# Layer 2's output product by Strassen's scheme: seven block products where there were eight

## The chip, the core and the metric

The kernel runs on one core of a Trainium2 chip. The metric is the device time of one execution in microseconds (us). Three runs of the kernel before gave 1030.38, 1031.73 and 1032.31 us; the median is 1031.73 us. The execution that the profiler recorded took 1031.0 us. Its span, from the first to the last instruction in the trace, is 1029.2 us, so 1.8 us of it lie outside the span.

Five engines work side by side, each with its own queue of instructions that it takes in order: PE (matrix products; a second row, PEld, lists its loads of the stationary operand), DVE (vector), ACT (scalar functions), POOL (general) and SP (issues the DMA transfers). Products are summed in PSUM, a small memory from which DVE and ACT read the result.

## The reference

Three stages run one after the other on 8 batches of 576 tokens. Attention with 8 heads over keys and values that are averaged in groups of 8 gives x with 512 features per token. Two gated layers follow. Layer 1:

```
h = relu(x @ w_in);  u, v = h[:, :512], h[:, 512:]       # w_in 512 x 1024
v_n = (v - mean(v)) / sqrt(var(v) + 1e-6)                # over the 512 features
v_s = w_spatial @ v_n + b_spatial                        # over the 576 tokens
x = (u * v_s) @ w_out                                    # w_out 512 x 512
```

Layer 2 has the same shape with other weights, a tanh form of GELU in place of relu, a gain on v_n, and the input added at the end: `x + gated @ w_out`. That last line is the product that is changed.

## The kernel before

**Numbers.** Every fp32 value that enters a product is split in two, a high part hi (rounded by ACT, L152) and a low part lo = value - hi (by DVE, in places by POOL, L153). A product is three products summed in one PSUM tile: hi by hi, hi by lo, lo by hi.

**Blocks.** A layer runs batch by batch, in blocks with one letter each in the strings that give the order. The layer's output is kept with features on the partitions (128 of them per tile) and 576 tokens along the row.
- `v`: 128 tokens by 512 features of the second half of h (`emit_v`, 12 matmuls of 512 columns, L252 to L254). Its chain on the other engines is GELU (L286, L287, L290, L291), the statistics (L300, L301, POOL L305 to L310), the gain (L321), hi (ACT L328) and lo (DVE L313). `v4` holds the last 64 tokens of two batches and so comes every second batch; its lo parts are 64 x 512.
- `u`: 128 features by 576 tokens of the first half (`emit_u`, L357, 24 matmuls of 288 columns), then GELU (L369, L370, L373, L374).
- `p`: the product with w_spatial for 128 features (`emit_sp`, L389, 28 matmuls of 288 columns). DVE multiplies it with u (L398) and the result gf is split into g (L152, L153).
- `o`: 128 output features (`emit_out`, L411, 4 feature chunks x 3 terms x 2 token halves = 24 matmuls of 288 columns). In layer 2 DVE adds the residual tile r (L422) and SP stores the result (L423). In layer 1 ACT copies it (L418) and SP stores it to x2d in DRAM, from which layer 2 loads it (`load_x`, `L`), splits it (`split_x`, `X`, lo on POOL) and gathers the last 64 tokens of two batches (`rem_x`, `R`).
- `G` loads and splits one of four 128 x 512 pieces of layer 2's w_out (`load_w2_out`), `I` pieces of its w_in, `E` its spatial weights.

**Order.** The emission order of layer 2 is written out in strings: PH2 for a batch in the steady state (the o blocks are those of the batch before), BOUND for the change from layer 1 to layer 2 and TAIL for the last batch. A scheduler keeps that as the order of priority on every engine, and a tile's number of buffers decides what waits: three PSUM tiles of two banks for u, p and o together, two PSUM tiles for v.

Of the kernel before, what the change touches and what calls it, by code (L numbers as in the profile page):

```python
# [32 lines left out]
SLAG = 0  # L33
LAG = {1: 4, 2: 2}
# [49 lines left out]
def attention_gmlp_gmlp(  # L84
# [40 lines left out]
    x2d = [[dram.tile([P, S], F32, name=f"x2d{b}_{c}") for c in range(NC)] for b in range(B)]  # L125
# [119 lines left out]
    seen = set()  # L245
    jobs_left = [2 * NC]
# [9 lines left out]
    def emit_v(layer, b, xt, t, pools, lag=1):  # L256
# [60 lines left out]
        def norm():  # L317
            if layer == 1:
                nc.vector.tensor_scalar(v[:m], v[:m], mv[:m, 0:1], None, ALU.subtract)
            else:  # L320
                nc.vector.scalar_tensor_tensor(  # L321
                    out=v[:m], in0=v[:m], scalar=mv[:m, 0:1], in1=pools["g"][:m],
                    op0=ALU.subtract, op1=ALU.mult,
                )
            if t < 4:
                o = pools["vn"].tile([P, 2, DH], F32R, tag="vn", name="vn")
                vn[b, t] = o
                nc.scalar.activation(out=o[:, 0], in_=v[:m], func=AF.Copy, scale=rstd[:m])  # L328
                lo_part(o[:, 1], o[:, 0], 0, m)
            elif not pair:  # L330
                hi = vna[b % 2][:m]
                nc.scalar.activation(out=hi, in_=v[:m], func=AF.Copy, scale=rstd[:m])
                nc.scalar.activation(out=vnx[b % 2][:m], in_=v[:m], func=AF.Copy, scale=rstd[:m])
                lo_part(vnx[b % 2][64:], hi, 0, m)
            else:
                hi = pools["h"].tile([P, DH], F32R, tag="h", name="h")
# [13 lines left out]

    def emit_u(layer, b, xt, d, pools):
        ps = ps_b.tile([P, 2, 512], F32, tag="b", name="pu")
        ds_ = slice(d * P, (d + 1) * P)
        for c in range(NC):
            for i, (w, hl) in enumerate(((wih, 0), (wih, 1), (wil, 0))):
                for h in range(2):
                    nc.tensor.matmul(  # L357
                        out=ps[:, h, :HALF], lhsT=w[c][:, ds_],
# [7 lines left out]
        else:  # L366
            sq = pools["w"].tile([P, S], F32, tag="squ", name="squ")
# [10 lines left out]
    def emit_sp(layer, b, d, pools):  # L378
        ps = ps_b.tile([P, 2, 512], F32, tag="b", name="psp")
        ds_ = slice(d * P, (d + 1) * P)  # L380
        seq = []
        for t in range(4):
            hi, lo = vn[b, t][:, 0, ds_], vn[b, t][:, 1, ds_]
            seq += [(hi, wsh[t]), (hi, wsl[t]), (lo, wsh[t])]
        seq.append((vna[b % 2][:97, ds_], wsa[:97]))
        seq.append((vnx[b % 2][:, ds_], wsx))
        for i, (l, r) in enumerate(seq):
            for h in range(2):
                nc.tensor.matmul(  # L389
                    out=ps[:, h, :HALF], lhsT=l, rhs=r[:, h * HALF:(h + 1) * HALF],  # L390
# [14 lines left out]
    def emit_out(layer, b, m, pools):  # L405
# [26 lines left out]
    if True:  # L432
# [34 lines left out]
        def mlp1(tok):  # L467
# [551 lines left out]
        w_p = ctx.enter_context(tc.tile_pool(name="w", bufs=2))  # L1019
        g_p = ctx.enter_context(tc.tile_pool(name="g", bufs=1))  # L1020
        r_p = ctx.enter_context(tc.tile_pool(name="r", bufs=8))
        xr_p = ctx.enter_context(tc.tile_pool(name="xr", bufs=2))
        h_p = ctx.enter_context(tc.tile_pool(name="h", bufs=1))
        staging.update(pool=ctx.enter_context(tc.tile_pool(name="stage", bufs=3)), tag="raw", n=S)
        gb = g_p.tile([P, DH], F32, name="gb")
        nc.sync.dma_start(out=gb, in_=g_ln.to_broadcast([P, DH]))
        pools.update({"w": w_p, "g": gb, "res": {}, "xr": {}, "h": h_p})
# [12 lines left out]
        def rem_x(b):  # L1040
            raw = xr_p.tile([P, NC, P], F32, tag="xw", name="xw")
            for i in range(2):
                for c in range(NC):
                    nc.sync.dma_start(out=raw[:, c, 64 * i:64 * i + 64], in_=x2d[b + i][c][:, 4 * P:])
            xr = xr_p.tile([P, 2, NC, P], F32R, tag="xr", name="xr")
            split(xr[:, 0], xr[:, 1], raw[:], nc.gpsimd)
            pools["xr"][b] = xr

        def mlp2(tok):
# [96 lines left out]
```

## Time and profile before

| what | value |
|---|---|
| median of three runs | 1031.73 us |
| profiled execution, and its span | 1031.0 us, 1029.2 us |
| PE busy over the span | 990.8 us (96%) |
| DVE, ACT, POOL busy | 669.4, 445.7, 441.9 us (65, 43, 43%) |
| DMA, mean rate over the span | 81 GB/s |
| clock granted to PE, mean of the run | 0.985 |

Attention and layer 1 take the first half of the span. Layer 1 of the last batch and layer 2 of the first overlap between about 490 and 575 us; from there to 1006 us layer 2 runs batch after batch, and the last 23 us are the last batch's output product. A share over the whole span mixes these stages, so the stages are shown apart in the rows below. Clock 1.00 means the upper one of PE's two levels, 2.4 GHz.

### The profile page before, as it was taken

The numbers are of one execution on the slowest core, as the hardware profiler recorded it, in microseconds if no ns is written. First come the engines' busy times: TensorE is split into PE (matmuls) and PEld (weight loads), VectorE is DVE, ScalarE is ACT, GpSimd is POOL, SyncE is SP. The second block draws the span as 40 slices with busy tenths as digits, with TensorE's granted clock in tenths as the row PEclk, the third lists the DMA queues.
The fourth block names the chain that finished last, engine by engine and source line by source line (L and its number), as shares of the span: only waits on it lengthen the run. The fifth ranks groups of instructions, "written<-read, shape, count | busy, mean of one in ns | idle before, by whom it ended". The sixth has DMA issues, their size and how long they took to land.

```text
span 1029.2 us, 17646 instructions
## 1 busy us (share of the span) xinstructions
PE 990.8 (96%) x6752; PEld 939.0 (91%) x6752; DVE 669.4 (65%) x1191; ACT 445.7 (43%) x849; POOL 441.9 (43%) x901
## 2 busy tenths in 40 slices
PE   7589889999999999999999999999999999999998
PEld 6469779999999999999999999999999999999998
DVE  5898867677676776766643477656665665556552
ACT  5564645435354353443533555333434343334330
POOL 4687657484674744714313234233322332232210
PEclk9689999999999999999999999999999999999999
DMA  8533343243332422222014312202011111111001
GB/s 276 169 122 107 121 130 111 88 122 97 104 100 77 138 70 66 83 70 70 30 44 134 109 56 67 70 24 80 24 48 46 48 46 46 46 47 47 12 13 69
DMA packets 49339, 83.00 MB, mean 81 GB/s; under 512 B 14052, under 2 KB 17124, under 8 KB 49256
## 3 DMA queue, kind: packets, MB, share of 16 engines
q1 hardware_dynamic: 49256, 81.89, 25.5%
q8 instruction: 53, 0.87, 0.4%
q14 instruction: 30, 0.25, 0.1%
HBM read 59.85 MB, written 22.02 MB: 80 GB/s over the span
## 4 chain that ended last, share of the span: by engine, by line
PE 82%; DVE 6%; DMA 4%; POOL 3%; ACT 3%; issue 1%; SPq 0%; POOLq 0%; DVEq 0%; ACTq 0%
PE psp L389 22%; PE pout L411 18%; PE pu L357 17%; PE pv L252 5%; PE pv L254 5%; PE pv L253 5%; PE psc L729 3%; DMA w2d_in<-dtmp 1%; POOL vr L597 1%; PE ptr L790 1%; DMA draw<-in_w_out_dram 1%; PE pv L265 1%; DMA vr<-in_v_dram 1%; PE ppv L252 1%; PE ppv L253 1%
## 5 line engine op out<-in xcount | busy, mean ns | idle before, releaser
L389 PE MATMUL psp<-wsh,vn 128*128 128x288 f32 x1024 | 189.9, 297 | 0.0
L411 PE MATMUL pout<-g,woh 128*128 128x288 f32 x1024 | 179.7, 297 | 2.7 <-DVE g L153 2.6
L357 PE MATMUL pu<-x,wih 128*128 128x288 f32 x1024 | 178.5, 296 | 0.0
L411 PEld LDWEIGHTS pout<-g,woh 128*128 128x128 f32 x1024 | 152.4, 189 | 5.5 <-DVE g L153 2.8
L389 PEld LDWEIGHTS psp<-wsh,vn 128*128 128x128 f32 x1024 | 153.7, 188 | 2.1 <-issue 1.0
L357 PEld LDWEIGHTS pu<-x,wih 128*128 128x128 f32 x1024 | 150.8, 188 | 1.3
L305 POOL TENSOR_SCALAR rs<-mv 128x1 f32<-128x1 f32 (+1 forms) x76 | 34.6, 455 | 189.0 <-DVE mv L301 186.6
L411 PE MATMUL pout<-g,wol 128*128 128x288 f32 x512 | 110.0, 296 | 0.0
L389 PE MATMUL psp<-wsl,vn 128*128 128x288 f32 x512 | 109.7, 295 | 0.0
L357 PE MATMUL pu<-x,wil 128*128 128x288 f32 x512 | 109.2, 295 | 0.0
L252 PE MATMUL pv<-wih,x 128*128 128x512 f32 x256 | 102.8, 402 | 3.0 <-ACT v L283 2.2
L152 ACT ACTIVATE g<-gf 128x576 fp32r<-128x576 f32 x64 | 43.9, 686 | 132.3 <-DVE gf L398 62.4
L254 PE MATMUL pv<-wih,x 128*128 128x512 f32 x256 | 100.9, 394 | 0.0
L253 PE MATMUL pv<-wil,x 128*128 128x512 f32 x256 | 100.6, 393 | 0.0
L153 DVE TENSOR_TENSOR g<-gf,g 128x576 fp32r<-128x576 f32 x64 | 56.3, 880 | 44.7 <-ACT g L152 44.6
L153 POOL TENSOR_TENSOR x<-r,x 128x576 fp32r<-128x576 f32 x32 | 47.5, 1486 | 84.9 <-ACT x L152 84.9
L411 PEld LDWEIGHTS pout<-g,wol 128*128 128x128 f32 x512 | 83.1, 190 | 0.0
L389 PEld LDWEIGHTS psp<-wsl,vn 128*128 128x128 f32 x512 | 82.5, 189 | 0.0
L357 PEld LDWEIGHTS pu<-x,wil 128*128 128x128 f32 x512 | 82.3, 189 | 0.0
L313 DVE SCALAR_TENSOR_TENSOR vn<-v,rs,vn 128x512 fp32r<-128x512 f32 x64 | 51.0, 799 | 43.9 <-ACT vn L328 43.9
L770 POOL TENSOR_TENSOR se<-se,sum 128x576 f32<-128x576 f32 (+1 forms) x35 | 41.9, 1196 | 65.6 <-DVE sum L769 64.9
L328 ACT ACTIVATE vn<-v,rs 128x512 fp32r<-128x512 f32 x64 | 45.7, 717 | 49.4 <-POOL rs L310 47.8
(177 smaller groups left out, 1968.1 us busy)
## 6 DMA issues: line engine op xcount, KB each, us to landing
x2d<-o SPq DMA_DIRECT2D x32, 288.0 KB, 3.0
r<-x2d SPq DMA_DIRECT2D x32, 288.0 KB, 3.1
out_dram<-o SPq DMA_DIRECT2D x32, 288.0 KB, 2.2
q<-in_qm_dram SPq DMA_DIRECT2D x32, 256.0 KB, 3.6
kr<-in_k_dram SPq DMA_DIRECT2D x14, 576.0 KB, 3.7
vr<-in_v_dram SPq DMA_DIRECT2D x28, 256.0 KB, 2.9
raw<-in_w_in_dram SPq DMA_DIRECT2D x8, 512.0 KB, 4.7
draw<-in_w_out_dram SPq DMA_DIRECT2D x16, 256.0 KB, 2.9
```

Source lines behind the costliest of these rows:

```text
L152: nc.scalar.activation(out=hi, in_=src, func=AF.Copy)
L153: (eng or nc.vector).tensor_tensor(out=lo, in0=src, in1=f32(hi), op=ALU.subtract)
L252: nc.tensor.matmul(out=o, lhsT=lh, rhs=rh, start=start and i == 0, stop=False)
L253: nc.tensor.matmul(out=o, lhsT=lh, rhs=rl, start=False, stop=False)
L254: nc.tensor.matmul(out=o, lhsT=ll, rhs=rh, start=False, stop=stop and i == n - 1)
L305: gp.tensor_scalar(a, mv[:m, 1:2], 1.0, eps, ALU.mult, ALU.add)
L313: nc.vector.scalar_tensor_tensor(out=lo, in0=v[r0:r1], scalar=rstd[r0:r1], in1=f32(hi), op0=ALU.mult, op1=ALU.subtract)
L328: nc.scalar.activation(out=o[:, 0], in_=v[:m], func=AF.Copy, scale=rstd[:m])
L357: nc.tensor.matmul(out=ps[:, h, :HALF], lhsT=w[c][:, ds_], rhs=xt[c][:, hl, h * HALF:(h + 1) * HALF], start=c == 0 and i == 0, stop=c == N ...
L389: nc.tensor.matmul(out=ps[:, h, :HALF], lhsT=l, rhs=r[:, h * HALF:(h + 1) * HALF], start=i == 0, stop=i == len(seq) - 1,)
L411: nc.tensor.matmul(out=ps[:, h, :HALF], lhsT=w[c][:, ms], rhs=gt[b, c][:, hl, h * HALF:(h + 1) * HALF], start=c == 0 and i == 0, stop=c == ...
L770: (nc.vector if (b, t) in SM_DVE else nc.gpsimd).tensor_tensor(e3, e3, sm[:m, :, None].to_broadcast([m, 8, SP]), ALU.mult)
```

## The change

The 512 x 512 product of a batch, out = A·B with A the transposed w_out and B the gated tile (features x tokens), is cut into 2 x 2 blocks: A into blocks of 256 x 256, B into blocks of 256 features x 288 tokens. The plain way takes eight block products. Now seven are computed, of sums and differences of blocks:

- S1 = A21+A22, S2 = S1-A11, S3 = A11-A21, S4 = A12-S2 are made once, when the weights are loaded: `load_w2_out` is called twice (before: four times), and each call loads two pieces, makes four 128 x 256 sums on POOL and splits seven 128 x 256 pieces on ACT and DVE.
- T1 = B12-B11, T2 = B22-T1, T3 = B22-B12, T4 = T2-B21 are made for each batch on POOL from the unsplit gf tiles (four 128 x 576 operations), and B11, B21, B22, T1, T2, T3, T4 are split: seven splits a batch, before four.
- The seven products `o0` to `o6` are 2 feature chunks x 3 terms x 2 = 12 matmuls of 288 columns each. Three PSUM tiles hold them. Tile a receives P1, and on top of it P6, P7 and P4 (o0, o2, o4, o6); tile d receives P5 and on top of it P3 (o1, o5); tile b receives P2 (o3). After each product DVE adds what the PSUM tile holds at that moment to one of four residual tiles, in place (seven additions a batch, L499 of the kernel after; before four).
- The residual is loaded from x2d once more for this (`load_r`, four transfers of 288 KB a batch), in blocks of 256 features x 288 tokens, and the stores have the same shape.
- u and p in layer 2 are computed in the same arrangement (`place`): a PSUM tile holds two 128-feature chunks of one token half, where it held two halves of one chunk. Neighbouring matmuls of a pair then have different stationary operands; before they had the same one.
- Layer 2's strings of order are new, and pools have other sizes (w 3, r 3, staging 4, residual 2 + 2, T tiles 2, shared with the tile of `rem_x`).

The core of the diff:

```diff
 PH2 = (
-    "v1 v0 o2 L0 v2 o0 L2 R o1 L3 v4 L1 u3 v3 u1 o3 X0 X1 u0 p1 p0 X3 u2 X2 p2 p3"
+    "o0 L2 v2 o1 L3 L1 v1 R o2 o3 v3 o4 X1 u0 o5 o6 L0 v0 v4 u1 X0 X3 u3 X2 u2 p1 p0 p3 p2"
 )
...
-    def load_w2_out(c):
-        seen.add(("G", c))
-        load_split(w2d_out[c][:, :], woh[c][:], wol[c][:])
+    def load_w2_out(k):
...
+            nc.gpsimd.tensor_tensor(o, x, y, op)
...
+            nc.scalar.activation(out=hi, in_=x, func=AF.Copy, scale=sg)
+            nc.vector.scalar_tensor_tensor(out=lo, in0=x, scalar=sg, in1=f32(hi), op0=ALU.mult, op1=ALU.subtract)
+            wblk[n, k] = hi, lo
...
+    def place(layer, d, j):
+        return (d, j) if layer == 1 else (d // 2 * 2 + j, d % 2)
...
-                for h in range(2):
+                for j in range(2):
+                    dd, h = place(layer, d, j)
                     nc.tensor.matmul(
-                        out=ps[:, h, :HALF], lhsT=w[c][:, ds_],
+                        out=ps[:, j, :HALF], lhsT=w[c][:, dd * P:(dd + 1) * P],
...
+        if layer == 2:
+            gb[b, GN[d]] = g
+            if GN[d] != "B12":
+                split_g(b, GN[d], "xg")
+            for o, x, y in TS:
+                if (b, o) not in gb and (b, x) in gb and (b, y) in gb:
+                    z = pools["t"].tile([P, S], F32, tag="raw", name="tf")
+                    nc.gpsimd.tensor_tensor(z, gb[b, x], gb[b, y], ALU.subtract)
+                    gb[b, o] = z
+                    if o in ("T1", "T2"):
+                        defer(TLAG, lambda o=o: split_g(b, o, "tg"))
+            return
...
+    PRODS = {
+        "5": ("S1", "T1", "d", "22"), "1": ("A11", "B11", "a", "11"), "2": ("A12", "B21", "b", "11"),
+        "6": ("S2", "T2", "a", "12"), "3": ("S4", "B22", "d", "12"), "7": ("S3", "T3", "a", "22"),
+        "4": ("nA22", "T4", "a", "21"),
+    }
...
+    def emit_out2(b, i):
...
+        wn, gn, pn, rn = PRODS[PORD[i]]
+        first = pn not in st
+        if first:
+            st[pn] = ps_b.tile([P, 2, 512], F32, tag="b", name="pout")
+        ps = st[pn]
...
+        for k in range(2):
+            hi, lo = wblk[wn, k]
+            for n, (w, hl) in enumerate(((hi, 0), (hi, 1), (lo, 0))):
+                for j in range(2):
+                    nc.tensor.matmul(
+                        out=ps[:, j, :HALF], lhsT=w[:, j * P:(j + 1) * P], rhs=two(g[:, hl])[:, k],
+                        start=first and k == 0 and n == 0, stop=k == 1 and n == 2,
...
+        if PORD[i] in "56":
+            split_g(b, "T3" if PORD[i] == "5" else "T4", "tg")
+        r = st[rn]
+        nc.vector.tensor_tensor(out=two(r[:]), in0=halves(ps), in1=two(r[:]), op=ALU.add)
...
-            r = pools["res"].pop((b, m))
-            nc.vector.tensor_tensor(out=two(o[:]), in0=halves(ps), in1=two(r[:]), op=ALU.add)
-            nc.sync.dma_start(out=out[b, ms, :], in_=o)
```

Where the instructions move, engine by engine. PE before, the steady state of layer 2: one whole output block `o` (g is the moving operand, woh and wol are the stationary high and low parts of w_out's four pieces).

```order
L411 MATMUL pout_10085<-g_9691,woh0_80 128x288 x4
L411 MATMUL pout_10085<-g_9691,wol0_84 128x288 x2
L411 MATMUL pout_10085<-g_9657,woh1_81 128x288 x4
L411 MATMUL pout_10085<-g_9657,wol1_85 128x288 x2
L411 MATMUL pout_10085<-g_9762,woh2_82 128x288 x4
L411 MATMUL pout_10085<-g_9762,wol2_86 128x288 x2
L411 MATMUL pout_10085<-g_9796,woh3_83 128x288 x4
L411 MATMUL pout_10085<-g_9796,wol3_87 128x288 x2
```

PE after, the same stage: o2 and o3 of one batch with the start of the v block behind them, then o4, the start of a u block, o5 and the start of o6 (pout_9866 is tile a, pout_9916 tile d, pout_9991 tile b; wx holds S2, S3 and S4).

```order
L490 MATMUL pout_9866<-g_9863,wx_6382 128x288 x12
L490 MATMUL pout_9991<-g_9858,woh2_82 128x288 x4
L490 MATMUL pout_9991<-g_9858,wol2_86 128x288 x2
L490 MATMUL pout_9991<-g_9858,woh3_83 128x288 x4
L490 MATMUL pout_9991<-g_9858,wol3_87 128x288 x2
L280 MATMUL pv_10010<-wih0_72,x_9639 128x512
...
L490 MATMUL pout_9866<-g_9933,wx_6382 128x288 x12
L388 MATMUL pu_10057<-x_9639,wih0_72 128x288 x4
...
L490 MATMUL pout_9916<-g_9817,wx_6382 128x288 x12
L490 MATMUL pout_9866<-g_9987,woh2_82 128x288 x4
```

An output block of 24 matmuls became products of 12, and tile a returns in every second one: between o2 and o4 lie o3 and a v block, between o4 and o6 a u block and o5.

DVE before, the steady state, the evacuation of a batch's four p blocks: gating (L398) and the low part (L153) of each, with a u block between the second and the third (L370, L374).

```order
L398 SCALAR_TENSOR_TENSOR gf_10183<-psp_10154,u_10079 128x576
L153 TENSOR_TENSOR g_10185<-gf_10183,g_10185 128x576
L398 SCALAR_TENSOR_TENSOR gf_10217<-psp_10188,u_10148 128x576
L153 TENSOR_TENSOR g_10219<-gf_10217,g_10219 128x576
L370 SCALAR_TENSOR_TENSOR squ_10251<-squ_10251,pu_10225 128x576
L374 SCALAR_TENSOR_TENSOR u_10250<-squ_10251,pu_10225 128x576
L398 SCALAR_TENSOR_TENSOR gf_10288<-psp_10259,u_10250 128x576
L153 TENSOR_TENSOR g_10290<-gf_10288,g_10290 128x576
L398 SCALAR_TENSOR_TENSOR gf_10322<-psp_10293,u_10018 128x576
L153 TENSOR_TENSOR g_10324<-gf_10322,g_10324 128x576
```

DVE after, the same place: the p blocks in the order p1, p0, p3, p2 (L429 gating, L155 low part; tf tiles are differences T made by POOL), and the first additions into the residual tiles (L499), between which the next batch's v blocks stand (L315, L319).

```order
L429 SCALAR_TENSOR_TENSOR gf_9779<-psp_9750,u_9504 128x576
L155 TENSOR_TENSOR g_9781<-gf_9779,g_9781 128x576
L429 SCALAR_TENSOR_TENSOR gf_9815<-psp_9786,u_9670 128x576
L155 TENSOR_TENSOR g_9817<-gf_9815,g_9817 128x576
L155 TENSOR_TENSOR g_9824<-tf_9784,g_9824 128x576
L429 SCALAR_TENSOR_TENSOR gf_9856<-psp_9827,u_9713 128x576
L155 TENSOR_TENSOR g_9858<-gf_9856,g_9858 128x576
L155 TENSOR_TENSOR g_9863<-tf_9820,g_9863 128x576
L499 TENSOR_TENSOR ro_9869<-pout_9866,ro_9869 128x576
L315 SCALAR_TENSOR_TENSOR sq_9900<-sq_9900,pv_9886 128x512
L499 TENSOR_TENSOR rrb_9867<-pout_9916,rrb_9867 128x576
L319 SCALAR_TENSOR_TENSOR v_9899<-sq_9900,pv_9886 128x512
```

The u block's evacuation is gone from between the p blocks, the splits of T1 and T2 came in, and an addition now stands among the next batch's v chain after every 12 matmuls.

## Rows read from the trace of the kernel before

**Rows 1.** Windows: length; busy us (count) PE, PEld, DVE, ACT, POOL; clock; DMA share.

```profile
492.00:575.00 83.00, 83.00 (x581) 79.32 (x580) 40.29 (x79) 34.35 (x65) 22.10 (x59) 1.00 0.21 64
575.00:1006.00 431.00, 431.00 (x2931) 413.13 (x2931) 263.79 (x402) 173.32 (x274) 129.21 (x255) 1.00 0.16 49
1006.00:1029.20 23.20, 19.30 (x145) 19.06 (x144) 6.07 (x8) 0.69 (x1) 0.00 (x0) 1.00 0.20 77
```

**Rows 2.** Windows, one stretch of two batches in layer 2, columns as before.

```profile
693.60:799.20 105.60, 105.60 (x718) 101.14 (x717) 62.49 (x97) 39.71 (x62) 32.18 (x64) 1.00 0.16 48
```

**Rows 3.** The chain that ended last: start us, length us, engine, tile, line, instructions.

```profile
674.50 3.20 PE pu L357 x24
677.70 7.45 PE psp L389 x56
...
704.47 0.24 PE pv L252
...
707.21 6.39 PE pout L411 x48
...
1006.11 19.20 PE pout L411 x144
```

**Rows 4.** Groups by line and shape: count, busy us, mean ns of one, idle before and releaser.

```profile
L411 PEld LDWEIGHTS pout<-g,woh 128*128 128x128 f32 x1024 | 152.4, 189 | 5.5 <-DVE g L153 2.8 <-PE psc L729 0.3
...
L153 DVE TENSOR_TENSOR g<-gf,g 128x576 fp32r<-128x576 f32 x64 | 56.3, 880 | 44.7 <-ACT g L152 44.6
...
L153 POOL TENSOR_TENSOR x<-r,x 128x576 fp32r<-128x576 f32 x32 | 47.5, 1486 | 84.9 <-ACT x L152 84.9
...
L152 ACT ACTIVATE g<-gf 128x576 fp32r<-128x576 f32 x64 | 43.9, 686 | 132.3 <-DVE gf L398 62.4 <-DVE gf L396 54.1 <-PE pu L357 15.8
...
L422 DVE TENSOR_TENSOR o<-pout,r 128x576 f32<-128x576 f32 x32 | 24.0, 749 | 13.1 <-PE pout L411 13.1
...
L597 POOL TENSOR_TENSOR vr<-vr 128x256 f32<-128x256 f32 x24 | 18.2, 759 | 16.6 <-DMA vr<-in_v_dram 12.0 <-DMA draw<-in_w_out_dram 4.4
...
L313 DVE SCALAR_TENSOR_TENSOR vnx<-v,rs,h 64x512 fp32r<-64x512 f32 x8 | 7.1, 890 | 0.2
...
L153 DVE TENSOR_TENSOR wol<-dtmp,woh 128x256 fp32r<-128x256 f32 x7 | 3.7, 522 | 0.6 <-ACT woh L152 0.5
...
L152 ACT ACTIVATE woh<-dtmp 128x256 fp32r<-128x256 f32 x8 | 3.3, 414 | 8.3 <-DVE dtmp L185 8.2
```

**Rows 5.** PE's timeline in layer 1, matmuls of 256 columns: start us, length, line.

```profile
437.41 0.28 PE L253 MATMUL ppv<-atT,vb 128*128 128x256 f32 x1
437.53 0.28 PE L254 MATMUL ppv<-atT,vb 128*128 128x256 f32 x1
437.65 0.28 PE L833 MATMUL ppv<-atR,vbr 96*128 96x256 f32 x1
```

**Rows 6.** Timeline of ACT and DVE, chains of a v and a u block.

```profile
978.52 0.60 ACT L286 ACTIVATE sq<-pv 128x512 f32<-128x512 f32 x1 [0.74 <-PE pv L254]
...
986.47 0.74 DVE L313 SCALAR_TENSOR_TENSOR vn<-v,rs,vn 128x512 fp32r<-128x512 f32 x1
...
988.10 0.65 ACT L369 ACTIVATE squ<-pu 128x576 f32<-128x576 f32 x1 [2.44 <-PE pu L357]
...
990.29 0.76 DVE L374 SCALAR_TENSOR_TENSOR u<-squ,pu 128x576 f32<-128x576 f32 x1 [0.75 <-ACT squ L373]
```

**Rows 7.** DVE's timeline at the end: last gating and low part, last addition.

```profile
1006.15 0.76 DVE L398 SCALAR_TENSOR_TENSOR gf<-psp,u 128x576 f32<-128x576 f32 x1 [1.45 <-PE psp L389]
1007.66 0.76 DVE L153 TENSOR_TENSOR g<-gf,g 128x576 fp32r<-128x576 f32 x1 [0.75 <-ACT g L152]
...
1025.34 0.76 DVE L422 TENSOR_TENSOR o<-pout,r 128x576 f32<-128x576 f32 x1 [2.44 <-PE pout L411]
```

**Rows 8.** DMA issues of the page: count, KB each, us to landing.

```profile
r<-x2d SPq DMA_DIRECT2D x32, 288.0 KB, 3.1
out_dram<-o SPq DMA_DIRECT2D x32, 288.0 KB, 2.2
```

More of the change, by code (lines that the diff above doesn't have):

```diff
@@ L33 @@
 SLAG = 0
+TLAG = 1
+PORD = "1562734"
 LAG = {1: 4, 2: 2}
@@ L124, in attention_gmlp_gmlp @@
     vnx = [act.tile([P, DH], F32R, name=f"vnx{i}") for i in range(2)]
-    x2d = [[dram.tile([P, S], F32, name=f"x2d{b}_{c}") for c in range(NC)] for b in range(B)]
+    x2d = [dram.tile([P, NC, S], F32, name=f"x2d{b}") for b in range(B)]
     w2d_in = [dram.tile([P, DFF], F32, name=f"w2d_in{c}") for c in range(NC)]
@@ L245, in attention_gmlp_gmlp @@
     seen = set()
+    wblk = {}
+    gb = {}
+    mid = {}
     jobs_left = [2 * NC]
@@ L335, in norm @@
             else:
-                hi = pools["h"].tile([P, DH], F32R, tag="h", name="h")
+                hi = pools["w"].tile([P, S], F32R, tag="sq", name="h")[:, :DH]
                 nc.scalar.activation(out=hi, in_=v, func=AF.Copy, scale=rstd)
@@ L366, in emit_u @@
         else:
-            sq = pools["w"].tile([P, S], F32, tag="squ", name="squ")
+            sq = pools["w"].tile([P, S], F32, tag="sq", name="squ")
             s2 = two(sq[:])
@@ L379, in emit_sp @@
         ps = ps_b.tile([P, 2, 512], F32, tag="b", name="psp")
-        ds_ = slice(d * P, (d + 1) * P)
         seq = []
         for t in range(4):
-            hi, lo = vn[b, t][:, 0, ds_], vn[b, t][:, 1, ds_]
+            hi, lo = vn[b, t][:, 0], vn[b, t][:, 1]
             seq += [(hi, wsh[t]), (hi, wsl[t]), (lo, wsh[t])]
-        seq.append((vna[b % 2][:97, ds_], wsa[:97]))
-        seq.append((vnx[b % 2][:, ds_], wsx))
+        seq.append((vna[b % 2][:97], wsa[:97]))
+        seq.append((vnx[b % 2], wsx))
         for i, (l, r) in enumerate(seq):
-            for h in range(2):
+            for j in range(2):
+                dd, h = place(layer, d, j)
                 nc.tensor.matmul(
-                    out=ps[:, h, :HALF], lhsT=l, rhs=r[:, h * HALF:(h + 1) * HALF],
+                    out=ps[:, j, :HALF], lhsT=l[:, dd * P:(dd + 1) * P], rhs=r[:, h * HALF:(h + 1) * HALF],
                     start=i == 0, stop=i == len(seq) - 1,
@@ L403, in emit_sp, with split_g @@
         split(o[:, 0], o[:, 1], g[:])
-    def emit_out(layer, b, m, pools):
+    GN = ("B11", "B12", "B21", "B22")
+    TS = (("T1", "B12", "B11"), ("T2", "B22", "T1"), ("T3", "B22", "B12"), ("T4", "T2", "B21"))
+    def split_g(b, n, tag):
+        o = pools[tag].tile([P, 2, S], F32R, tag=tag, name="g")
+        gt[b, n] = o
+        split(o[:, 0], o[:, 1], gb[b, n][:])
+    PRODS = {
+        "5": ("S1", "T1", "d", "22"), "1": ("A11", "B11", "a", "11"), "2": ("A12", "B21", "b", "11"),
+        "6": ("S2", "T2", "a", "12"), "3": ("S4", "B22", "d", "12"), "7": ("S3", "T3", "a", "22"),
+        "4": ("nA22", "T4", "a", "21"),
+    }
@@ new lines, in load_r, with store @@
+    def load_r(b, mi, h, tag):
+        r = pools[tag].tile([P, S], F32, tag=tag, name="r" + tag)
+        nc.sync.dma_start(out=two(r[:]), in_=x2d[b][:, 2 * mi:2 * mi + 2, h * HALF:(h + 1) * HALF])
+        return r
+    def store(b, mi, h, o):
+        nc.sync.dma_start(
+            out=out[b, 256 * mi:256 * mi + 256, h * HALF:(h + 1) * HALF].rearrange("(j p) s -> p j s", p=P), in_=two(o[:])
+        )
+    def emit_out2(b, i):
+        assert i == 0 or (b, "o", i - 1) in seen
+        seen.add((b, "o", i))
+        st = mid.setdefault(b, {})
+        wn, gn, pn, rn = PRODS[PORD[i]]
[3 more added lines that the diff above has]
+        ps = st[pn]
+        if i == 0:
+            st["22"], st["11"] = load_r(b, 1, 1, "rb"), load_r(b, 0, 0, "o")
+        elif i == 1:
+            st["12"], st["21"] = load_r(b, 0, 1, "rb"), load_r(b, 1, 0, "o")
+        g = gt.pop((b, gn))
+        for k in range(2):
+            hi, lo = wblk[wn, k]
+            for n, (w, hl) in enumerate(((hi, 0), (hi, 1), (lo, 0))):
+                for j in range(2):
+                    nc.tensor.matmul(
+                        out=ps[:, j, :HALF], lhsT=w[:, j * P:(j + 1) * P], rhs=two(g[:, hl])[:, k],
+                        start=first and k == 0 and n == 0, stop=k == 1 and n == 2,
+                        skip_group_check=not first,
+                    )
+        if PORD[i] in "56":
+            split_g(b, "T3" if PORD[i] == "5" else "T4", "tg")
+        r = st[rn]
+        nc.vector.tensor_tensor(out=two(r[:]), in0=halves(ps), in1=two(r[:]), op=ALU.add)
+        st[rn, "n"] = st.get((rn, "n"), 0) + 1
+        if st[rn, "n"] == (1 if rn == "21" else 2):
+            store(b, int(rn[0]) - 1, int(rn[1]) - 1, r)
@@ L1017, in attention_gmlp_gmlp @@
                 run(steady(STEADY, b), phase1)
-        w_p = ctx.enter_context(tc.tile_pool(name="w", bufs=2))
+        w_p = ctx.enter_context(tc.tile_pool(name="w", bufs=3))
         g_p = ctx.enter_context(tc.tile_pool(name="g", bufs=1))
[L1021 to L1027, printed above, removed]
+        r_p = ctx.enter_context(tc.tile_pool(name="r", bufs=3))
+        rb_p = ctx.enter_context(tc.tile_pool(name="rb", bufs=2))
+        tg_p = ctx.enter_context(tc.tile_pool(name="tg", bufs=2))
+        wx_p = ctx.enter_context(tc.tile_pool(name="wx", bufs=1))
+        t_p = ctx.enter_context(tc.tile_pool(name="stage", bufs=4))
+        staging.update(pool=t_p, tag="raw", n=S)
+        wx = wx_p.tile([P, 3, 2, 2, 256], F32R, name="wx")
+        gln = g_p.tile([P, DH], F32, name="gln")
+        nc.sync.dma_start(out=gln, in_=g_ln.to_broadcast([P, DH]))
+        pools.update({"w": w_p, "g": gln, "res": {}, "xr": {}, "rb": rb_p, "tg": tg_p, "t": t_p, "wx": wx, })
         def load_x(b, cs):
@@ L1065, in mlp2 @@
                     seen.add((1, "o", B + b, i))
-                    emit_out(1, B + b, i, pools)
+                    emit_out(B + b, i, pools)
                 else:
-                    assert all(("G", c) in seen for c in range(NC))
-                    emit_out(2, b, i, pools)
+                    assert all(("G", c) in seen for c in range(2))
+                    emit_out2(b, i)
             elif k == "E":
```

48 lines of the change are left out of this document (33 added, 15 removed), and 8 rows, old and new, of the table BOUND.

## The prediction

> **What bounds the kernel now.** I first read the busy time by stage. From 492 us to 1006 us PE is busy for 83.00 of 83.00 and 431.00 of 431.00 us, at clock 1.00 [rows 1]. In one stretch of two batches it is again 105.60 of 105.60 us, while DVE is busy for 62.49 (59%), ACT for 39.71 (38%), POOL for 32.18 (30%) and the DMA engines for a share of 0.16 [rows 2]. So in the part of the program that the change touches PE sets the time, and the others have room. The chain of waits says the same: in layer 2 it runs from one PE piece to the next, and at the end 144 matmuls of the output product stand in a row, 19.20 us [rows 3]. That last piece has 19.30 us of PE in a window of 23.20; the rest is what follows the last product, one DVE addition and a store [rows 1, 7].
>
> A matmul of 288 columns costs 19.20/144 = 0.1333 us in a stream, whichever block it is in: u takes 3.20 for 24, p takes 7.45 for 56, the output product 6.39 for 48 [rows 3]. A v block is 12 matmuls of about 0.24, some 2.8 us.
>
> **What goes.** The output product of a batch falls from 96 matmuls to 84, over 8 batches 96 fewer. Each lies in a stage where PE has no gap, so 96 x 0.1333 = 12.8 us leave the path. Everything up to the last batch's layer 1 keeps its order on every engine, so the time before about 500 us stays.
>
> **What comes, beside PE.** For each batch:
> - DVE: three more splits of 0.77 and three more additions of 0.75 (the size of the last rows; the means over the run are 0.88 and 0.749) [rows 4, 7], 4.6 us. Two batches then need 62.5 + 9.2 = 71.6 us of a stretch that shrinks to 105.6 - 24 x 0.1333 = 102.4, that is 70%.
> - ACT: three hi parts of 0.686 [rows 4], 43.8 of 102.4 us for two batches.
> - POOL: four differences. The trace has no such operation; the POOL low part has the same size, 1.486 us [rows 4]. Two batches: 32.2 + 11.9 = 44.1 us, 43%.
> - DMA: four more loads of 288 KB, which landed 3.1 us after issue [rows 8]. They are issued at o0 and o1 into tiles that the batch before has long stored, and the share of 0.16 leaves room.
>
> All of that is hidden by PE as long as no PE instruction has to wait. So the question is which new waits end late.
>
> **Wait 1: tile a is read between its products.** o2 may not write until DVE has added o0's sum, and so on. PE before the addition and after it: between o0 and o2 lie two v blocks and o1 (2.8 + 1.6 + 2.8 = 7.2 us), between o2 and o4 lie o3 and a v block (4.4), between o4 and o6 a u block and o5 (3.2 + 1.6 = 4.8). An addition takes 0.76, and it starts at once when DVE is free: the last one starts 0.03 us after the matmuls end at 1025.31 [rows 3, 7]. Even behind three other DVE operations of 0.76 it ends 3.1 us after the product. Cost 0. Were all of the cover gone, the price would be some 0.9 us three times a batch (a rival below). What queues behind a late o2, o4 or o6 is the whole of PE.
>
> **Wait 2: T3 and T4 are split late.** Their splits are issued behind o1 and o2 (0.686 + 0.77 us, 1.5 with the hand-over), and o4 and o6 come at least 4.4 us later. Where the T tile is shared with the 64-token tile of two batches, T4's split must wait for o4 to end, and has 4.8 us. Cost 0.
>
> **Wait 3: from the v blocks to p.** The new order puts the last v block of a batch before three u blocks, then p begins. Before the first p needs v's low part PE works for 3 x 3.20 + 4 x 0.1333 = 10.1 us. The second of two adjacent v blocks took from 978.5 (product's end) to 987.2 (low part's end), 8.7 us [rows 6]: 1.4 us to spare. In every second batch the 64-token block stands between, and its parts are needed only at the 25th matmul of p, 9.6 + 3.2 = 12.8 us later. On DVE, however, the GELU of two of the three u blocks stands ahead of its low part. The second u ends at 6.4 us, its GELU takes from 988.01 to 991.05, 3.0 us [rows 6], and the low part of 64 x 512 takes 0.89 [rows 4]: 10.3 us, 2.5 to spare, of which ACT and POOL work in that chain may take half. Cost 0, bound 0.75 us (one DVE operation more) in every batch, 6 us.
>
> **Wait 4: the change of layers, once.** The two G calls put on POOL 8 operations of 128 x 256 (0.759 each, 6.1 us), on ACT 14 hi parts (0.414, 5.8 us) and on DVE 14 low parts (0.522, 7.3 us) [rows 4], between the last layer-1 output block and the first product of layer 2, where PE has two u and four p blocks: 6.4 + 14.9 = 21.3 us. That fits. The three v blocks in a row there wait for two PSUM tiles, and the third one has about nothing to spare. I take 0.3 us, bounds 0 and 1.5.
>
> **Wait 5: the end.** The last batch's seven products stand almost together, so o4 follows o2 by only one product (1.6 us) while the addition needs 0.8, with a T split perhaps ahead of it on DVE (0.77). The last p block takes 2.3 us from its end to its low part (1006.11 to 1008.42) [rows 3, 7], and two products of 1.6 cover it. I take 0.1, bounds 0 and 1. The last addition and the last store stay. The store landed in 2.2 us in rows of 2304 bytes [rows 8]; the new one has twice as many rows of half that length. The trace has no store of that shape: between 0.2 us less and 0.9 us more (the 3.1 us of the load of the same size); I take 0.2.
>
> **The stationary operands.** In layer 2 every matmul of u, p and o now has another stationary operand than its neighbour; before, pairs shared one: (96 + 112 + 84)/2 = 146 matmuls a batch, 1168 in all, newly change it. The trace before lists one load for each matmul already (1024 for 1024), of 189 ns each, longer than the pace of 133 ns [rows 4]. So the loads run beside matmuls and beside each other. In layer 1 matmuls of 256 columns whose operand changes from one to the next start 0.12 us apart (437.41, 437.53, 437.65) [rows 5]. Cost 0; bounds 0 and 1168 x (0.189 - 0.133) = 65 us, and I stay at the end that the rows show directly.
>
> The Trainium skill, "TensorE: Matmul & The Clock Gate", says in the section "The mechanism" of its Part 3 that a weight load overlaps with running matmuls only where its row group differs, and in "LDWEIGHTS (loading the stationary operand)" that a load of P columns takes about P/1.2 ns, so 107 ns for 128. By that rule alone these full-height loads would each stand between matmuls, and the estimate by those pages would be 1168 x 0.107 = 125 us more if a load of the same operand were free. The rows disagree with it: 0.12 us from start to start holds no such load.
>
> **The sum.** Span 1029.2 - 12.8 + 0.3 + 0.1 + 0.2 = 1017.0 us, execution 1017.0 + 1.8 = 1018.8. The median of the runs, 1031.73, stands 0.7 above the profiled 1031.0, so on that scale the forecast is 1019.5. With all waits at their lower ends it is 1031.7 - 12.8 - 0.2 = 1018.7, and on the profiled execution's scale 1018.0. With the upper ends of waits 4 and 5 and the store it is 1018.9 + 1.5 + 1 + 0.9 = 1022.3.
>
> **Rivals.**
> 1. The seam between v and p comes late. DVE is at 70% and its order is fixed, so an addition that waits for PE holds back the v chain behind it; three residual additions now stand inside it. Against it: 1.4 us and 2.5 us to spare. The price is 0.75 us or so in each of 8 batches, 6 us: 1025.5.
> 2. Slower: the changed stationary operands set the pace. For it: 189 ns of loading against 133 ns of pace, and PEld is busy for 413 of 431 us [rows 1]. Against it: the 0.12 us of rows 5. It decides once the 1168 matmuls need over 0.1333 + 12.2/1168 = 0.144 us; at 0.189 the time is 1019.5 + 65 = 1084.
> 3. Slower too: tile a's reads are exposed, because the scheduler or the hardware keeps DVE's addition behind more than it seems. Three waits of some 0.9 us gain nothing back: 24 x 0.9 = 22, so 1041. Against it: 4.4 us of other products at the tightest place, in the order itself.
> 4. The change does not do what it says: the matmul count on PE falls by 96 in the order, so only its price is open. No chance is given to it.
>
> **Chances.** Forecast as summed 0.82, rival 1 0.12, rival 2 0.03, rival 3 0.03. A difference of 0.2% (2.1 us) is about what a measurement of this kernel can tell from none. The forecast and most of rival 1 lie below 1029.6: faster 0.92. The worse tails of rival 1 give 0.02 for the same; rivals 2 and 3 together are slower, 0.06. The range runs from 1017.5 (no wait at all, the lower bound of the store and 0.5 for the spread of runs) to 1025 (nearly all of rival 1).
>
> **What would show it.** Right: PE again without a gap in layer 2, a two-batch stretch of 102.4 us, a product of 12 matmuls in 1.6 us, the additions of tile a ended at least 2 us before the next product, DVE near 70% there. Wrong: PE idle time before o2, o4 or o6 that DVE's addition ends (rival 3), or before a p block that a low part ends (rival 1); or u, p and o matmuls more than 0.134 us apart with no wait shown (rival 2). If the two-batch stretch shortens by 3.2 us and the time does not, the loss is at the change of layers or at the end.

## The result and the profile after

The changed kernel took 1020.08 us (median of 4 runs, 1015.35 to 1023.53) against 1032.02 us (4 runs) before: a ratio of 0.988, with a 95% interval from 0.984 to 0.993. The forecast was 1019.5 us. The profiled execution took 1021.6 us; its span is 1019.8 us.

The windows of the kernel after, columns as in [rows 1, 2], and all waits of PE from 480 us on (who waited for whom: us, times, longest):

```profile
575.00:1006.00 431.00, 430.19 (x2927) 411.56 (x2926) 321.25 (x459) 185.36 (x306) 182.46 (x294) 1.00 0.25 74
...
696.00:798.40 102.40, 102.40 (x695) 97.87 (x694) 76.78 (x109) 42.38 (x68) 44.01 (x73) 1.00 0.25 73
```

```profile
PE pu L388 <- DVE ro L499: 0.7, 1, 0.7
PE pout L490 <- DVE g L155: 0.5, 1, 0.5
PE pout L490 <- DVE rrb L499: 0.5, 1, 0.5
```

PE has no gap in the steady state, at clock 1.00. The length of the second window is the one that was forecast for two batches, not a measurement; two batches are measured from one p block to the same one two batches later. PE's timelines of before, then of after:

```profile
681.00 0.43 PE L389 MATMUL psp<-wsx,vnx 128*128 128x288 f32 x2
...
786.57 0.43 PE L389 MATMUL psp<-wsx,vnx 128*128 128x288 f32 x2
```

```profile
685.08 0.43 PE L420 MATMUL psp<-wsx,vnx 128*128 128x288 f32 x2
...
787.29 0.43 PE L420 MATMUL psp<-wsx,vnx 128*128 128x288 f32 x2
```

That is 105.57 us before and 102.21 after, 3.36 less; the 24 matmuls were forecast at 3.20. DVE is higher than forecast, 76.8 us and not 71.6. Three short waits came, 1.7 us in all; the forecast had 0.4.

Executions differ by some us ahead of layer 2, so I also use a stretch that leaves this out: from the last pair of matmuls of the p block at 575 us to the last matmul of the program. (That block is layer 1's, of the last batch: DVE gates it at L396. Layer 1 runs to about 626 us, and layer 2's first v block stands at 590; the bounds of 490 and 575 us given ahead of the rows are too early.) PE's timelines of before, then of after:

```profile
578.54 0.43 PE L389 MATMUL psp<-wsx,vnx 128*128 128x288 f32 x2
...
1024.87 0.43 PE L411 MATMUL pout<-g,wol 128*128 128x288 f32 x2
```

```profile
579.86 0.43 PE L420 MATMUL psp<-wsx,vnx 128*128 128x288 f32 x2
...
1015.39 0.42 PE L490 MATMUL pout<-g,wol 128*128 128x288 f32 x2
```

From start to the last end that is 446.8 us before and 435.9 us after, 10.8 less: 12.8 less for the matmuls, 1.7 more for the waits, and 0.3 more that this sum leaves open. A version without any of the three waits (`t_dve`, below) has 433.4, 13.3 less than before; measured against it, the three waits of 1.7 us cost 2.5. In two further executions of the kernel after the same stretch is 436.0. The stretch began 1.3 us later than before. The runs below, with the same instructions ahead of it, began it at 577.7 to 583.6 us, so I take this for the spread of executions and not for the change. After the last matmul come one addition and one store, 4.0 us (before 3.9), so the new store shape costs about 0.1.

### The profile page after: what moved, and what is told of

It is laid out like the page before. It is cut to its first block, busy times and chain, and to the rows that moved or that the text cites. A ratio compares the mean times of both kernels' runs of the same rounds, so it can differ in the third digit from the quotient of the medians.

```text
span 1019.8 us, 17703 instructions
## 1 busy us (share of the span) xinstructions
PE 979.1 (96%) x6656; PEld 925.9 (91%) x6656; DVE 726.3 (71%) x1249; ACT 459.2 (45%) x883; POOL 497.4 (49%) x941
## 4 chain that ended last, share of the span: by engine, by line
PE 76%; DVE 12%; DMA 4%; ACT 4%; POOL 3%; issue 2%; SPq 0%; DVEq 0%; POOLq 0%; ACTq 0%
PE psp L420 20%; PE pu L388 17%; PE pout L510 8%; PE pout L490 7%; PE pv L280 5%; PE pv L281 5%; PE pv L282 5%; PE psc L823 3%; DVE g L155 1%; DMA w2d_in<-dtmp 1%; PE pv L293 1%; PE ptr L884 1%; DMA draw<-in_w_out_dram 1%; PE ppv L280 1%; DVE sum L861 1%
## 5 line engine op out<-in xcount | busy, mean ns | idle before, releaser
L154 ACT ACTIVATE g<-gf 128x576 fp32r<-128x576 f32 x56 | 38.4, 686 | 157.6 <-DVE gf L429 86.7
L333 POOL TENSOR_SCALAR rs<-mv 128x1 f32<-128x1 f32 (+1 forms) x76 | 32.5, 428 | 131.3 <-DVE mv L329 128.6
L510 PE MATMUL pout<-g,woh 128*128 128x288 f32 x512 | 91.1, 300 | 3.3 <-DVE g L155 3.2
L155 DVE TENSOR_TENSOR g<-gf,g 128x576 fp32r<-128x576 f32 x56 | 63.7, 1137 | 40.9 <-ACT g L154 40.8
L510 PEld LDWEIGHTS pout<-g,woh 128*128 128x128 f32 x512 | 76.8, 191 | 5.2 <-DVE g L155 3.6
L155 POOL TENSOR_TENSOR x<-r,x 128x576 fp32r<-128x576 f32 x32 | 47.6, 1496 | 59.6 <-ACT x L154 51.3
L691 POOL TENSOR_TENSOR vr<-vr 128x256 f32<-128x256 f32 (+5 forms) x108 | 56.8, 528 | 23.3 <-DMA vr<-in_v_dram 12.3
L328 DVE BATCH_NORM_STATS2 st<-v 128x6 f32<-128x512 f32 (+1 forms) x76 | 52.0, 684 | 21.8 <-ACT v L311 15.9
```

Of the source, the lines that this page charges most:

```text
L155: (eng or nc.vector).tensor_tensor(out=lo, in0=src, in1=f32(hi), op=ALU.subtract)
L328: nc.vector.bn_stats(st[:m], v[:m])
L510: nc.tensor.matmul(out=ps[:, h, :HALF], lhsT=w[c][:, ms], rhs=gt[b, c][:, hl, h * HALF:(h + 1) * HALF], start=c == 0 and i == 0, stop=c == ...
L691: nc.gpsimd.tensor_tensor(t[:m, :n], t[:m, :n], t[:m, n:2 * n], ALU.add)
```

## The experiments

In the order of the argument. "Stretch" is the one just described.

**Is the gain the matmuls alone?** `eight` puts the 96 matmuls back and leaves everything else:

```diff
-        for k in range(2):
+        ks = (0, 1, 0, 1) if PORD[i] == "2" else (0, 1)
+        for q, k in enumerate(ks):
...
```

> The changed kernel with the product P2 (o3) computed twice into its tile, so that a batch has 96 matmuls again; the output holds P2 twice. All additions, splits, differences, loads and new order stay. Theory (PE bound, side work hidden): 96 x 0.133 = 12.8 us slower than the changed kernel, about 1032.5, which is the kernel before within 2 us, and a two-batch stretch of 105.6 us. Rival (part of the gain comes from the new order or from the arrangement of u and p, or the side work costs and o3's extra 1.6 us cover it): 1022 to 1028.

1034.1 us, ratio to the kernel before 1.0003 [0.9986, 1.0020]; stretch 447.0. A window as long as the forecast for two batches, then the two rows of PE's timeline that measure them:

```profile
696.00:801.60 105.60, 105.60 (x720) 101.07 (x719) 77.11 (x109) 42.49 (x68) 43.77 (x72) 1.00 0.24 71
```

```profile
689.40 0.43 PE L420 MATMUL psp<-wsx,vnx 128*128 128x288 f32 x2
...
794.79 0.43 PE L420 MATMUL psp<-wsx,vnx 128*128 128x288 f32 x2
```

Two batches take 105.39 us, with 77 us of DVE in place of 62 [rows 2] and no gap on PE. So in the steady state all of the side work is hidden. Of the 3.36 us, 3.18 are the matmuls; the other 0.18 stay when the matmuls are back, so they belong to the new order or arrangement, and which of them is not shown. `eight` also has only one of the three waits, of 0.5 us.

**Do changed stationary operands cost?** `alt_weights` edits the kernel before: in layer 2 the second matmul of each pair takes the next 128-column block, (d + h) % 4. The edit in u; those in p and the output product are alike:

```diff
-                        out=ps[:, h, :HALF], lhsT=w[c][:, ds_],
+                        out=ps[:, h, :HALF], lhsT=w[c][:, other(layer, d, h)],
...
```

> The kernel before, with one edit: in layer 2 the second matmul of each pair of u, p and output product takes the stationary operand of the next 128-column block, so that it is no longer that of the first (1216 matmuls change their operand newly); layer 2 therefore mixes blocks. Nothing else moves. Theory (a load runs beside matmuls whether or not it brings the same operand): 1032 us, no difference, a two-batch stretch of 105.6 us. Rival (changed operands set the pace, 0.189 us a load): up to 1216 x 0.056 = 68 us slower, about 1100.

1032.98 us, ratio 0.9996 [0.9980, 1.0012]:

```profile
696.00:801.60 105.60, 105.60 (x719) 101.14 (x718) 62.49 (x96) 39.74 (x63) 32.31 (x64) 1.00 0.16 48
```

No difference, in the stretch either (446.8 in both). Rival 2 is refuted, and these loads do not follow the rule of the Trainium skill ("TensorE: Matmul & The Clock Gate", "The mechanism") that the prediction weighed.

**The kernel after, again.**

Six more runs, for a narrower interval and as the measure for the edits below.

> The changed kernel unedited, as the measure for the others on the same chip and for a narrower interval. Theory (PE sets the time of layer 2, 96 matmuls of 0.133 us go, 1.7 us of new waits come): 1018.5 to 1021.5 us, a ratio of about 0.989 to the kernel before. If the 2.8 us by which the first profile's span stays short of the forecast were a fixed cost of the change, the stretch up to the last output block of layer 1 (x2d stored at 541.5 us, before 540.2 us) is again 1.3 us later; if it is only the spread of executions, it lies between 539 and 543 us without a rule.

1022.65 us, ratio 0.9894 [0.9876, 0.9913]; the waits are the same three (0.8, 0.5, 0.5), the stretch is 436.0. It began at 579.6 us; in `alt_weights`, where the kernel before runs ahead of it, it began at 581.4, so no fixed delay of the change shows ahead of it.

**What does a reuse of tile a cost without cover?** `b2b` moves the seven products together:

```diff
-    "o0 L2 v2 o1 L3 L1 v1 R o2 o3 v3 o4 X1 u0 o5 o6 L0 v0 v4 u1 X0 X3 u3 X2 u2 p1 p0 p3 p2"
+    "o0 o1 o2 o3 o4 o5 o6 L2 v2 L3 L1 v1 R X1 u0 v3 L0 v0 v4 u1 X0 X3 u3 X2 u2 p1 p0 p3 p2"
```

> The changed kernel with the seven products of a batch in a row in the steady state (o0 to o6, then v, v, u, v, v and on), so that only one product of 1.6 us lies between two uses of tile a, as at the end of the program. Theory: o2 waits for the first addition, which stands behind the gating and a low part on DVE, 1 to 1.3 us in each of 7 batches, the later ones next to nothing: 7 to 12 us slower than the changed kernel, 1028 to 1032. Rival 3 of the prediction (a read of tile a costs 0.9 us at each reuse, cover or not): 7 x 3 x 0.9 = 19 us here and no less in the changed kernel. If the scheduler had hidden nothing by its order, no difference.

1052.6 us, ratio 1.018 [1.016, 1.020]: 30 us slower than the kernel after, more than either theory. PE's timeline of `b2b`, and windows around that wait:

```profile
708.42 3.22 PE L490 MATMUL pout<-g,wx 128*128 128x288 f32 x12 [2.27 <-DVE ro L499]
711.44 0.81 PE L490 MATMUL pout<-g,woh 128*128 128x288 f32 x4
```

```profile
706.10:708.40 2.30, 0.05 (x1) 0.01 (x1) 2.30 (x4) 0.69 (x2) 0.22 (x1) 0.97 0.32 71
708.40:710.00 1.60, 1.58 (x7) 1.60 (x7) 1.21 (x2) 0.00 (x0) 0.00 (x0) 0.50 0.10 23
710.00:712.00 2.00, 2.00 (x11) 2.00 (x11) 0.32 (x1) 0.28 (x1) 0.00 (x0) 0.58 0.00 0
```

The place was foreseen: o2 waits for the first addition, behind gating and low parts on DVE. It is 2.3 us and not 1 to 1.3: the low part ahead of the addition took 1.37 us (why, below), and the split of T2, 0.74, stood there too. And behind the gap PE runs at clock 0.50, its lower level of 1.2 GHz, for over 3 us: 12 matmuls take 3.0 us where they take 1.6. One such wait stands in each of six batches (2.3 us in five; in the first 2.6, for which the listing names no releaser), 6 x (2.3 + 1.4) = 22 of the 30 us; other waits of the listing (3.2 us before v, 2.0 for a split) make most of the rest. So rival 3's reads do cost where the cover is gone, and the written order with v and u between the products is what makes this change faster.

**How much room is there from v to p?** `seam` moves u1 ahead of the last v block:

```diff
-... o5 o6 L0 v0 v4 u1 X0 X3 u3 X2 u2 p1 p0 p3 p2
+... o5 o6 L0 u1 v0 v4 X0 X3 u3 X2 u2 p1 p0 p3 p2
```

> The changed kernel with one block moved in the steady string: u1 in front of the last v block instead of behind it, so that two u blocks (6.4 us) and not three lie between v and p. Theory (the prediction's wait 3: a chain of 8.7 us against 10.1 us of cover): 6.9 us of cover are 1.8 us too few in the batches without a 64-token block, which are 3 of the 6 that this string orders: 3 x 1.8 = 5.4 us slower than the changed kernel (1022.6), about 1028. If a wait of this length also lowers PE's clock, as the 2.3 us wait of the run with the products in a row did (12 matmuls in 3.0 instead of 1.6 us behind it), 3 x 3.3 = 10 us, about 1033. Rival (the chain has far more room than 1.4 us): no difference.

1045.1 us, ratio 1.012 [1.009, 1.015]; the stretch is 458.2, 22 us longer than in the kernel after: the expected 5 to 10 fell short. Rows of its PE timeline, of a batch without and one with the 64-token block, then POOL's, then a window behind the first of these waits:

```profile
684.64 0.53 PE L420 MATMUL psp<-wsh,vn 128*128 128x288 f32 x2 [2.38 <-ACT vn L356]
...
739.53 0.80 PE L420 MATMUL psp<-wsh,vn 128*128 128x288 f32 x4 [0.46 <-DVE vn L341]
743.73 0.54 PE L420 MATMUL psp<-wsa,vna 97*128 97x288 f32 x2 [1.26 <-POOL vna L368]
```

```profile
678.64 3.30 POOL L155 TENSOR_TENSOR x<-r,x 128x576 fp32r<-128x576 f32 x2 [8.55 <-ACT x L154]
681.91 0.19 POOL L333 TENSOR_SCALAR rs<-mv 128x1 f32<-128x1 f32 x1
```

```profile
684.40:687.40 3.00, 2.75 (x18) 2.53 (x19) 1.66 (x3) 1.99 (x4) 1.43 (x1) 1.00 0.00 0
```

PE's waits add up to 18.5 us, some in every steady batch. In the second execution of the kernel after (`again`), v's low part ends 1.4 us before p reads it in the first batch without the 64-token block, 2.1 us in the next two and 0.5 us in the last batch; the low part of the 64-token block ends at 736.09, and the 27th matmul of p, the first that reads it, starts at 737.32, 1.2 us later. The expectation counted only the lost cover. With u1 gone from behind v0, the small POOL operations of v0's statistics also stand behind two low parts of x on POOL (3.3 us); in the kernel after they come before them. The waits do not add up to the loss: from p block to p block two batches take 109.3 us, 7.1 more, and the five waits listed in them make 5.2. Behind the wait of 2.38 us the clock stayed at 1.00; why it fell in `b2b` and not here is open.

**How near is DVE?** `add2` repeats each addition:

```diff
         nc.vector.tensor_tensor(out=two(r[:]), in0=halves(ps), in1=two(r[:]), op=ALU.add)
+        nc.vector.tensor_tensor(out=two(r[:]), in0=halves(ps), in1=two(r[:]), op=ALU.add)
```

> The changed kernel with every one of the seven additions done twice in a row (the output holds each sum twice): DVE gets 5.2 us more a batch and rises from 77 to about 87 of 102.4 us in two batches, and PSUM tile a is released 0.75 us later each time. Theory (PE bound, slack of 1.4 us and more in the steady state): the two-batch stretch grows by less than 1 us; at the end of the program each reuse of tile a waits 0.75 us longer and the last addition is 0.75 us later, 2 to 3 us: 1024 to 1027. Rival (DVE is the near bound, what is added shows): 5.2 x 7 = 36 us, 1059.

1040.3 us, ratio 1.007 [1.004, 1.010]; the stretch is 453.9, 18 us longer. Neither number is met. PE's timeline of `add2`, a long window, and one behind the last wait:

```profile
771.94 1.82 PE L490 MATMUL pout<-g,wx 128*128 128x288 f32 x12 [1.33 <-DVE rrb L500]
773.93 0.77 PE L388 MATMUL pu<-x,wih 128*128 128x288 f32 x4 [0.17 <-DVE ro L500]
...
1028.45 4.84 PE L490 MATMUL pout<-g,wx 128*128 128x288 f32 x24 [3.17 <-DVE rrb L500]
```

```profile
695.50:804.50 109.00, 106.68 (x720) 101.09 (x719) 87.99 (x125) 43.19 (x69) 44.69 (x73) 1.00 0.24 68
...
1028.45:1030.00 1.55, 1.55 (x6) 1.55 (x7) 0.52 (x1) 0.00 (x0) 0.00 (x0) 0.50 0.06 19
```

DVE is busy for 87.99 of 109.00 us here, 81%, not full, and PE waits all the same, 0.8 or 1.5 us a batch, 3.4 us in the first and 3.2 at the end, each of these two with a lower clock behind it. An addition that becomes ready late stands behind v's chain in DVE's order. So room on DVE is not what its busy share suggests.

**Why are the splits long?** `t_dve` moves the T differences from POOL to DVE:

```diff
-                    nc.gpsimd.tensor_tensor(z, gb[b, x], gb[b, y], ALU.subtract)
+                    nc.vector.tensor_tensor(out=z, in0=gb[b, x][:], in1=gb[b, y][:], op=ALU.subtract)
```

> The changed kernel with the four differences T of a batch made by DVE instead of POOL. In the changed kernel DVE's splits beside a POOL difference take 1.38 and 1.97 us, without one 0.75. If the two engines hold each other up, all splits fall to 0.75 to 0.77 and DVE's two-batch total stays at 77 us or rises by less than 3 in spite of eight more operations of 0.75 (6 us); if the long splits have another reason (the operands' place), they stay and the total rises to 83. Time: within 2 us of the changed kernel either way, since PE has no wait there.

Groups of the splits and differences in layer 2, of the kernel after and then of `t_dve`:

```profile
L155 DVE TENSOR_TENSOR g<-gf,g 128x576 fp32r<-128x576 f32 x27 | 33.7, 1247 | 20.3 <-ACT g L154 20.3
L155 DVE TENSOR_TENSOR g<-tf,g 128x576 fp32r<-128x576 f32 x30 | 32.3, 1076 | 0.1
L439 POOL TENSOR_TENSOR tf<-gf 128x576 f32<-128x576 f32 x16 | 27.0, 1689 | 39.0 <-DVE gf L429 39.0
```

```profile
L155 DVE TENSOR_TENSOR g<-tf,g 128x576 fp32r<-128x576 f32 x32 | 24.0, 750 | 0.1
L155 DVE TENSOR_TENSOR g<-gf,g 128x576 fp32r<-128x576 f32 x28 | 21.3, 761 | 4.5 <-ACT g L154 4.5
L439 DVE TENSOR_TENSOR tf<-gf 128x576 f32<-128x576 f32 x16 | 12.1, 755 | 0.3
```

```profile
696.00:798.40 102.40, 102.40 (x694) 97.84 (x693) 76.56 (x117) 42.43 (x68) 31.53 (x64) 1.00 0.25 73
```

The splits fall from 1.25 and 1.08 to 0.76 and 0.75 us, and DVE's total for two batches stays at 76.6 us with eight operations more. So POOL's differences cost DVE as much as the differences themselves. PE has no wait at all from 480 us to the end; the stretch is 433.4 us, 2.5 less than that of the kernel after, a little more than the 2 expected. The time is 1017.9 us, ratio 0.9855 [0.9825, 0.9885]. The Trainium skill, "SBUF — State Buffer", states in its section "SBUF: two separate sides" that a DVE operation with two SBUF inputs and a GpSimd operation that reads SBUF exclude each other, so that the later one waits for the whole of the other. The rows agree: in the steady state of the kernel after, a split that began beside a POOL difference of 1.44 us took 1.38, the one behind it, beside a difference of 1.94, took 1.97 or 1.98, and each ended 0.6 us after that difference; additions and gating, with one input in PSUM, stay at 0.72 to 0.76. One such pair, from DVE's and POOL's timelines:

```profile
695.85 1.98 DVE L155 TENSOR_TENSOR g<-tf,g 128x576 fp32r<-128x576 f32 x1
```

```profile
695.27 1.94 POOL L439 TENSOR_TENSOR tf<-gf 128x576 f32<-128x576 f32 x1
```

**The end alone.** `tail` makes only T4 of the last batch on DVE and emits the first addition of tile d behind that of tile a (of the edit, the line that makes T4):

```diff
+            nc.vector.tensor_tensor(out=z[:], in0=gb[b, "T2"][:], in1=gb[b, "B21"][:], op=ALU.subtract)
```

> The changed kernel with T4 of the last batch made by DVE in the gap between gating and low part, and the first addition of tile d issued behind that of tile a there. Theory (the last block's low part takes 1.44 instead of 0.75 us because POOL makes T4 at the same time, and o3 and o4 wait for it and for what stands behind it): the wait of 0.50 us before the second term of o3 goes, the one before o4 stays at or under 0.5, and the end comes 0.5 to 1.0 us earlier: 1021.6 to 1022.1 on this chip's scale of 1022.6, less than the runs can tell, so it is read in the trace. If the low part is long for another reason, the 0.50 us stays.

The wait of 0.50 us before o3's second term is gone, the one before o4 stays at 0.5, and the stretch is 435.3, 0.6 less. 1020.9 us, ratio 0.9891 [0.9868, 0.9914]: in the runs alone it can't be told.

**The version with T on DVE beside the kernel after**, on one chip:

> The version with the T differences on DVE again, on the same chip as the changed kernel and with more rounds, to tell whether it is the faster one. Theory (1.8 us of waits go, with what PE loses behind them; all waits in layer 2 were DVE's splits made long by POOL): 2 to 4 us below the changed kernel, ratio to the kernel before 0.985 to 0.987. Rival (the 1017.9 us were the spread of four runs): within 1 us of the changed kernel.

> The changed kernel beside it on the same chip: 1020 to 1023 us, ratio 0.988 to 0.990, 1.8 us of waits in the trace again.

1019.4 us, ratio 0.9874 [0.9849, 0.9900], against 1021.4 us, 0.9891 [0.9863, 0.9919]. The difference is 2.0 us and the intervals overlap, so the runs alone do not tell the two apart. The stretch does, 433.5 against 436.0 us, within 0.1 us the numbers of the executions before. Against the kernel before, this version is 1.3 to 1.5% faster.

## Why the prediction was right, and where its terms were off

- **The number:** 1020.1 against 1019.5 us is closer than the terms were. On the stretch 12.4 us less were forecast (12.8 for the matmuls, 0.3 and 0.1 for waits 4 and 5) and 10.8 came, and the interval of the ratio reaches 4.5 us to either side; that the two agree within 0.6 us is partly luck.
- **The matmuls:** right. 96 x 0.133 = 12.8 us; with `eight` the stretch is within 0.2 us of that before, and its one wait of 0.5 us is in that.
- **Stationary operands:** right, at the end of the range that the rows showed; `alt_weights` measured it. The count of 1168 was too low: a high part served four matmuls in a row before, not two, so some 1536 matmuls of the kernel after newly change theirs. Only the upper bound hung on it.
- **DVE's added work:** mis-sized. The splits were priced at 0.77 us from rows in which POOL stood still; beside POOL's new differences they take 1.08 to 1.25 on average. Two batches need 76.8 us and not 71.6, 75% of their time and not 70. The mean of 0.88 in [rows 4], which was set aside, was a sign of it: in the kernel before, every split g<-gf longer than 1 us stood beside a POOL operation, as here DVE's and POOL's:

```profile
591.68 1.03 DVE L153 TENSOR_TENSOR g<-gf,g 128x576 fp32r<-128x576 f32 x1 [0.75 <-ACT g L152]
```

```profile
590.66 1.43 POOL L153 TENSOR_TENSOR x<-r,x 128x576 fp32r<-128x576 f32 x1
```

- **Waits 1 to 4:** cost 0 in the steady state, as taken. At the place with the least cover, in the second execution, o2's addition ends at 759.93 and o4 starts at 763.30, 3.4 us later. But the tightest place is o4's addition in every second batch, which stood behind v's chain on DVE; DVE's and PE's timelines there:

```profile
767.38 0.75 DVE L499 TENSOR_TENSOR rrb<-pout,rrb 128x576 f32<-128x576 f32 x1
```

```profile
769.64 0.69 PE L490 MATMUL pout<-g,woh 128*128 128x288 f32 x4
```

  It ends at 768.13 and o6 starts 1.5 us later; in the first batch and the last but one the least room is 0.6. So the sign that was named, at least 2 us, did not hold, though nothing waited. The change of layers cost nothing (0.3 was taken): PE shows no wait there. One wait was not forecast: in the first batch u, which takes the PSUM tile of o3 in the ring of three, waited 0.7 us for o3's addition.
- **Wait 5:** 1.0 us and not 0.1. The last p block's low part ran beside T4 on POOL, DVE's and POOL's timelines of the kernel after:

```profile
1007.23 1.44 DVE L155 TENSOR_TENSOR g<-gf,g 128x576 fp32r<-128x576 f32 x1 [0.75 <-ACT g L154]
...
1009.92 0.74 DVE L499 TENSOR_TENSOR rrb<-pout,rrb 128x576 f32<-128x576 f32 x1
```

```profile
1006.62 1.43 POOL L439 TENSOR_TENSOR tf<-tf,gf 128x576 f32<-128x576 f32 x1 [2.76 <-DVE gf L429]
```

  POOL ends at 1008.05 and DVE's low part 0.62 us later, at 1008.67, as if it had begun only then. In [rows 7] the same low part took 0.76 us. In `t_dve` it does so again, and neither of the two waits is there.
- **The rivals:** the two on DVE's side (1 and 3) did not come true, but were priced too low. A wait was counted at its own length. `b2b` shows one of 2.3 us that costs 3.7, and `seam` and `add2` show that one instruction's delay meets others in the queues: 18 to 22 us came of edits for which 2 to 10 were expected. Had the order been a little tighter, the change would have been slower, as `b2b` and `seam` are.

## What to carry to other kernels

Where one engine is busy without a gap, instructions taken from it are worth their pace, and all other work is free until an order makes that engine wait. Here a wait then cost more than its length, so judge the room at each hand-over and not by the busy share of the engine that serves it. Before giving POOL more work beside a busy DVE, price DVE's operations with two SBUF inputs at more than their time alone (here 0.75 us became 1.38 to 1.99); doing the work on DVE itself may cost no more.

## What the runs showed that was not expected

- After 2.3 us without matmuls PE's granted clock was 0.50 for over 3 us, in all of the six batches of `b2b`, and it fell as well behind the 3.4 and 3.2 us of `add2`; after gaps of 2.38 us in `seam` it was 1.00. What decides between them was not tried.
- A DVE operation with two inputs in SBUF took 1.38 to 1.99 us instead of 0.75 beside a POOL operation of 1.43 to 1.95 us, and POOL's took 1.94 instead of 1.43 where it began beside such a split.
- The stretch from the p block at 575 us to the last matmul repeats within 0.1 us in the profiled executions of one kernel (three of the kernel after, two of `t_dve`), while its start varies by 6 us among all profiled executions, and whole times by up to 8 us. That all of the spread lies before the stretch is shown for the profiled executions only.
